# Attention over a key/value cache: one of five P tiles of every second step transposed by DMA instead of TensorE

## Chip, core and metric

The kernel runs on one core of a Trainium2 chip. The metric is the device time of one execution in microseconds; a lower time is better. The kernel before takes 722.17 us, the median of three runs (721.92 to 722.21).

## What is computed

Two independent problems, A and B, of the same shape are computed, and their outputs are set side by side. All arrays are bf16.

```python
# x (16, 80, 576), k_cache and v_cache (16, 16, 512, 128), wq (576, 4096), wo (4096, 576)
q = (x @ wq).reshape(16, 80, 32, 128).transpose(0, 2, 1, 3)     # 32 query heads
k, v = jnp.repeat(k_cache, 2, axis=1), jnp.repeat(v_cache, 2, axis=1)   # 16 cached heads, 2 query heads each
p = softmax(einsum("bhqd,bhkd->bhqk", q, k) * 128 ** -0.5)
o = einsum("bhqk,bhkd->bhqd", p, v)
out = o.transpose(0, 2, 1, 3).reshape(16, 80, 4096) @ wo         # (16, 80, 576)
```

## The kernel before

The work is cut into 128 steps, numbered U: one step is one batch element with four cached heads (so eight query heads) of one problem. Its 8 x 80 = 640 query rows make five tiles of 128 rows by 512 keys. Tiles k = 1 to 4 hold the first 128 of the 160 rows of each cached head. Tile k = 0, the remainder tile, holds the last 32 rows of each of the four heads, 4 x 32 = 128 rows. A step goes through these operations:

- The K load (`em_ldk`, L626) is a transposing DMA for two steps at once, into one of six buffers (`NK`); the V load (`em_ldv`, L630) is a plain DMA for one step. Both are issued by SyncE (SP), as are the loads of `wq`, `wo`, `x` and the stores of the output (`em_st`, L851).
- The query projection (`em_qp`, L537) multiplies `wq` by the transposed `x`. The last 64 of the 576 rows of the contraction are done by `em_qt` (L550) as two matmuls on the two 64-row halves of the array, side by side. A projection that belongs to a step U of at least `US0` has its `em_qt` pair put at the head of that step's transposes; an earlier one is an instruction pair of its own.
- The scores are `em_qk` (L673, full array, 512 columns) for tiles 1 to 4 and `em_qkr` (L660, four 32-column strips) for the remainder tile. From the third step on the remainder tiles of two neighbouring steps are scored together.
- The softmax of a tile is a maximum on VectorE (L682), an exponential with its row sum on ScalarE (L686), a reciprocal on VectorE (L692), for tiles 0 to 2 and 3 to 4 together, and the normalisation on GpSimd (POOL, `em_nrm`, L695), which writes the P tile in SBUF.
- The transposes (`em_tr`, L727) turn the five P tiles on TensorE into PSUM: 40 instructions, in pairs on the two 64-row halves of the array. Two copies per step (`em_ptev`, L738 on ScalarE or L740 on VectorE) bring tiles 1 to 4 into `pT` in SBUF, and two more (`em_prev`, L745 or L747) bring the remainder tile. `pT` has two blocks (`NPT`), used by even and odd steps.
- P·V (`em_pv`, L770) is four groups of four matmuls with V as the stationary and 160 columns of `pT` as the moving operand. The result goes to `oT` (L784).
- The output projection (`em_op`, L816) multiplies `oT` by `wo`; copies and additions (L828, L845) and the stores end it.

Nothing is scheduled at run time. Every operation is added to a list with its engine, the tiles it reads and writes, and a stream name, and the table `ORDER` gives the order of all of them, with the PSUM bank of each result and, where an apostrophe stands, ScalarE in place of VectorE for a copy. The letters stand for the streams in alphabetical order. Each engine takes its operations in that order. Waits on semaphores are derived from the reads and writes, and every DMA waits in SP's one queue:

```python
for op in ops:
    if op.eng != name:
        continue
    for ck, v in op.waits:
        e.wait_ge(sem_of(ck), v)
    inst = op.emit(e, name) if op.alt else op.emit(e)
```

Of the kernel before, what the change touches and what calls it, by code (L numbers as in the profile page):

```python
# [18 lines left out]
NPT = 2  # L19
# [11 lines left out]
US0 = 2  # L31
# [16 lines left out]
XLD = ((-100.0, -60.0), (-5.0, -4.9))  # L48
# [11 lines left out]
LETTERS = "abcdefghijklmnopqrstuvwxyzABCDEFGHIJKLMNO"  # L60
ORDER = """
nEKni7KHHHHHHNj3Ej4IMk5j6MNIj7j3Mk4ILd6Id5IIdd2AaBd1dd5BAd6dd2'Bd1dd6BMd0AdAd7'BAd5Ldd4'A'Bd6dd5'ABKMd7add3'AB
d4e0doe1'Be2'Ad5ole7of6ld3ole0pe1dlod4omd2Ke7A'BhdCloe6vhf5Cald3oud0lBupf12luAdme7puo'BOmg0456Cpu'Ae1y'wOe3'xl
vj0oj4d5'zuCMj7loe6ud0moue1dMlk2Md4Llok7e2c3'AFBcle6hod5a'sLldog0137'BAe2'yCd5CCvw'zoj3e0lue7Mj4o'xve3lc6Mcuc1
locuof24ld0tu'spc7lucpg16muCtme3uzd2'youe7e6'wd4'xho'AFlg15oalBc3Cz'xe0u'wcle7Bc5uoc'yf46v'ACsle1oud2'tpd3ulc5
omcpg07lCsuc4'yCze1e5'wvmcob7u'Aolue0te2'xe6olhud4hoblholae0Bd5lCove1f23'qolug67Cplud0wumzc1cpu'yc7e2'Axe6smcd
4o'BCg13olutle5uc2xCco'zue7c6'sBd3vlwoe2e4u'ycCod5'Aulhtc1e0huoclag67sloe1'zc2yc'xlCf47Coud6'tBv'wle0pe2c5uAcm
c1ouc'se3od4'tulpg15vlob0'wCyluxe2'zAue1bomhColaue6e7d3oluc5Be2'qocle0d4Colug16sluof57'zvyd2lCpc6u'wc'xp'Ae0uc
1md3Bo'tcmg45hF'se6'yxe1hCBc7u'zFe4oclae5vb3olute0lwboolc7Ce1olud6Acluc4qcCovd3se0ulg25Cou'tf17'yxuCBe4'zd2wvp
lc3d5uAmoe0ucpg16'sulob3wlze4A'ye6bhCouholavc2d1q'xulcd3tme0Bf26og45plpc7mcyd0'wme2sc4oc'ze7d6C'txulBc4cou'Ae5  # L70
c3'socle1g24o'thlChCe7uxb3'who'yua'Ae2le5uoe0b'zuolCe1Bd4ulod6vloc7ue2lCqcc5ovlcg03slCtvf17y'zue2'xCb3p'Buwmpc
6ucAbmuo'sue0le1hoc7ud4'qhold3hae2lcCovg56'tluf01y'zub7w'xCpu'Be2Ambuople0c3oc'qc4'se2d5loce7C'td3vole0ug46lub
2'zCymohb'wJxBGe1'qc7oJcle2hc3Ald4hoe0acClod5vsg16lu'tuf27C'zwyb3u'xpuc6AmcuBe0e1oe4uc5bsloc'qd6tle0od3oe1lg25
olCb4pu'zxmwue0ye5blvABd6oc7ohle1e2Jqd3lGochg04slJof57a'w'yAc1pcb6'tCCx'zvle0d4uo'Be1c2umocd3ule5buloCslug01Cp
'quc2w'x'ye6Aue5cmod4u'zte0d7o'Ble1og23loc6'wCcylud5az'sue2'Ac0xe6lCocuc3'BcCv'toc4e1lcuod7'tlsuf02lg34upmb6y'
zwhpe0'xd3'AaComue1e5c4Blvcoc2c'svod7lute0le4og12ole5bxz'ylCoe0ud2'w'BAc4ule1Cod3v'qhcolc7uhe6Chcloug05h'tsuhl
f17xauB'ye4e6p'wb3'zpmc5od0mocle1Ad7slg24CouCc6'yzvce5'xC'te2wvd4ole6oulboule1Bc5ulAce2oud7'qoc3ulcCsg06lu'tuf
15z'w'ye2pb3'x'Bhomc7hCAculae0e1od4ubplComuc6e0qd2luog35slCuf17x'yBc'wu'zpe0d3'tomc5cCpc6u'Ae2le1scvod4'tvog05
lhuhle6zb2a'yCoume1we0vod5'x'Bc7Aulcoc4cld3t'se6e1log47ole0bCCo'wulzud6'x'yBe1u'Ae7Coc4ld3uo'qe5hvclag02sulof1
4u'wxlAc7cp'yb6p't'ze0e7moe2c5cBlbCouod3lvCc1slue0qcd5omuhhf27tlug46pe0y'wb1'zC'xou'Be6mFbvolue2qc4'Ae5olcac3s  # L80
d1CCpcud4'toulg06vb3'wzluA'xue2me6Bboyld4oe1Fc7od5lhqg02lf36'wz'Ae1xcCoc4u'sce2Blhud7od5'tp'ye1Ke4lob0mCoue2bl
puolvg13lc4z'ycc2q'se1acmoe0e4b3xlCCou'td6Bulwd2ovg15AluCf07w'zCve4'ype5b'AuomFoue1lKc6xd0uKo'qe4lhd3uolcuBc5c
# [184 lines left out]
def bass_concat_heads__gqa_block_cached__gqa_block_cached__near_ridge_kernel(  # L267
# [27 lines left out]
    with ExitStack() as es:  # L295
# [634 lines left out]
```

## Time and profile before

| | |
|---|---|
| median of three runs | 722.17 us |
| the profiled execution | 722.56 us |
| its span, first to last instruction | 720.6 us |
| TensorE clock granted | 1.0 of full speed |
| TensorE matmuls busy | 715.3 us (99%) |
| VectorE, ScalarE, GpSimd busy | 641.3, 639.8, 432.6 us |
| DMA bytes moved | 160.73 MB, mean 223 GB/s |

The profile is one execution. An engine's busy time is the time in which it had an instruction in work; matmuls overlap in TensorE's pipeline, so the mean time of one is longer than the distance from one to the next. "Idle before" is the time for which an engine had nothing in work before an instruction, with the engine and line that ended it. The chain of the profile follows the work back from the last instruction, at each step to what released it. For a DMA, the issue is the time of the instruction in SP's queue, and the landing is counted from the start of the issue to the semaphore.

### The profile page before, as it was taken

The numbers are of one execution on the slowest core, as the hardware profiler recorded it, in microseconds if no ns is written. First come the engines' busy times: TensorE is split into PE (matmuls) and PEld (weight loads), VectorE is DVE, ScalarE is ACT, GpSimd is POOL, SyncE is SP. The second block draws the span as 40 slices with busy tenths as digits, with TensorE's granted clock in tenths as the row PEclk, the third lists the DMA queues.
The fourth block names the chain that finished last, engine by engine and source line by source line (L and its number), as shares of the span: only waits on it lengthen the run. The fifth ranks groups of instructions, "written<-read, shape, count | busy, mean of one in ns | idle before, by whom it ended". The sixth has DMA issues, their size and how long they took to land.

```text
span 720.6 us, 26290 instructions
## 1 busy us (share of the span) xinstructions
PE 715.3 (99%) x10820; PEld 513.1 (71%) x10820; DVE 641.3 (89%) x1459; ACT 639.8 (89%) x1844; POOL 432.6 (60%) x650
## 2 busy tenths in 40 slices
PE   9999999999999999999999999999999999999998
PEld 5567767777677777777777777777777777777777
DVE  3999998899888998899998899979999889998995
ACT  1999999799989998789997899989999889998993
POOL 0477755566556675665675567646676656755773
PEclk9999999999999999999999999999999999999999
DMA  9999999899999999999999998999999898988860
GB/s 248 268 269 259 265 255 241 206 189 259 225 241 209 217 254 240 226 254 205 268 207 219 248 245 212 247 236 204 181 262 224 193 241 198 220 194 200 178 199 18
DMA packets 374167, 160.73 MB, mean 223 GB/s; under 512 B 278560, under 2 KB 370976, under 8 KB 374048
## 3 DMA queue, kind: packets, MB, share of 16 engines
q1 hardware_dynamic: 374048, 159.05, 95.6%
q8 instruction: 86, 1.41, 0.8%
q14 instruction: 33, 0.27, 0.1%
HBM read 87.65 MB, written 2.95 MB: 126 GB/s over the span
## 4 chain that ended last, share of the span: by engine, by line
PE 98%; ACT 1%; issue 0%; DVE 0%
PE ps L816 22%; PE ps L770 20%; PE ps L537 19%; PE ps L673 16%; PE ps L727 11%; PE ps L660 5%; PE ps L550 4%; ACT p_sb L686 1%; PE ps L348 0%; PE ps L396 0%; ACT qT L563 0%; PE ps L414 0%; PE ps L451 0%; DVE osb L845 0%; DVE wo_sb L341 0%
## 5 line engine op out<-in xcount | busy, mean ns | idle before, releaser
L695 POOL TENSOR_SCALAR p_sb<-p_sb,rinv 128x512 bf16<-128x512 bf16 x640 | 430.8, 694 | 272.7 <-DVE rinv L692 272.2
L686 ACT ACTIVATE p_sb<-ps,negmax 128x512 bf16<-128x512 f32 x640 | 444.0, 711 | 29.8 <-DVE negmax L682 25.5
L682 DVE TENSOR_REDUCE negmax<-ps 128x1 f32<-128x512 f32 x640 | 419.2, 681 | 27.5 <-PE ps L673 22.2
L770 PE MATMUL ps<-pT,v_sb 128*128 128x160 bf16 x2048 | 191.1, 233 | 0.1
L770 PEld LDWEIGHTS ps<-pT,v_sb 128*128 128x128 bf16 x2048 | 154.0, 98 | 39.5 <-ACT pT L745 3.3
L816 PE MATMUL ps<-wo_sb,oT 128*128 128x288 bf16 x1280 | 181.6, 286 | 0.0
L673 PE MATMUL ps<-kT,qT 128*128 128x512 bf16 x512 | 176.4, 381 | 0.0
L537 PE MATMUL ps<-xT,wq_sb 128*128 128x320 bf16 x1024 | 176.0, 299 | 0.0
L816 PEld LDWEIGHTS ps<-wo_sb,oT 128*128 128x128 bf16 x1280 | 122.1, 98 | 43.2 <-ACT p_sb L686 1.7
L686 ACT ACTIVATION_READ_ACCUMULATOR p_sb<-ps,negmax 128x1 f32 x640 | 144.0, 225 | 0.0
L537 PEld LDWEIGHTS ps<-xT,wq_sb 128*128 128x128 bf16 x1024 | 94.5, 98 | 42.4 <-ACT p_sb L686 2.2
L727 PEld LDWEIGHTS ps<-ident,p_sb 64*128 64x128 bf16 x5120 | 91.4, 95 | 8.8 <-issue 1.1
L727 PE MATMUL ps<-ident,p_sb 64*128 64x64 bf16 x5120 | 96.1, 190 | 1.2 <-ACT qT L563 0.7
L738 ACT COPY pT<-ps 128x512 f32<-128x512 f32 x150 | 88.4, 603 | 9.4 <-PE ps L727 9.0
L740 DVE COPY pT<-ps 128x1024 bf16<-128x1024 bf16 x106 | 72.0, 684 | 13.2 <-PE ps L727 11.7
L563 ACT ACTIVATE qT<-ps 128x320 bf16<-128x320 f32 x131 | 59.5, 462 | 16.2 <-PE ps L550 15.4
L784 DVE CAST oT<-ps 128x320 bf16<-128x320 f32 x129 | 61.5, 482 | 6.5 <-PE ps L770 6.0
L564 DVE TENSOR_SCALAR qT<-ps 128x320 bf16<-128x320 f32 x125 | 59.5, 482 | 8.1 <-PE ps L550 6.6
L673 PEld LDWEIGHTS ps<-kT,qT 128*128 128x128 bf16 x512 | 48.4, 97 | 25.7 <-issue 3.3
L784 ACT CAST oT<-ps 128x320 bf16<-128x320 f32 x127 | 56.4, 448 | 10.2 <-PE ps L770 9.9
L745 ACT COPY pT<-ps 128x128 f32<-128x128 f32 x132 | 36.1, 288 | 7.0 <-PE ps L727 6.8
L692 DVE RECIPROCAL rinv<-rowsum 128x3 f32<-128x3 f32 (+1 forms) x256 | 39.5, 161 | 2.3 <-ACT p_sb L686 2.2
(31 smaller groups left out, 194.7 us busy)
## 6 DMA issues: line engine op xcount, KB each, us to landing
v_sb<-in_A_v_cache_dram SPq DMA_DIRECT2D x64, 512.0 KB, 5.4
v_sb<-in_B_v_cache_dram SPq DMA_DIRECT2D x64, 512.0 KB, 4.9
wo_sb<-in_A_wo_dram SPq DMA_DIRECT2D x8, 576.0 KB, 5.6
wo_sb<-in_B_wo_dram SPq DMA_DIRECT2D x8, 576.0 KB, 5.6
wq_sb<-in_B_wq_dram SPq DMA_DIRECT2D x4, 1024.0 KB, 6.6
out_dram<-osb SPq DMA_DIRECT2D x40, 72.0 KB, 3.4
wq_sb<-in_A_wq_dram SPq DMA_DIRECT2D x8, 256.0 KB, 4.5
wq_sb<-in_A_wq_dram SPq DMA_DIRECT2D x2, 1024.0 KB, 7.3
```

Source lines behind the costliest of these rows:

```text
L537: last = e.matmul(ps[:, vbq[h].phys, QO:QO + 320], lhsT=wq_sb[:, wsl, ck, hi * 128:(hi + 1) * 128], rhs=xT[:, half, ck, n0:n0 + 320], star ...
L563: return e.activation(dst, src, AF.Identity, scale=SCALE)
L673: return e.matmul(ps[:, vb.phys, :], lhsT=qT[:, qsl, bl, gl * 160:gl * 160 + 128], rhs=k_of(U, gl), start=True, stop=True)
L682: return e.tensor_reduce(negmax[:, si:si + 1], ps[:, vb.phys, :], axis=AX.X, op=AluOpType.max, negate=True)
L686: return e.activation(p_sb[:, psl, :], ps[:, vb.phys, :], AF.Exp, bias=negmax[:, si:si + 1], scale=1.0, accum_out=rowsum[:, ss, k:k + 1])
L695: return e.tensor_scalar(p_sb[:, psl, :], p_sb[:, psl, :], rinv[:, ss, k:k + 1], 1.0, op0=AluOpType.mult, op1=AluOpType.mult)
L727: last = e.matmul(dst, lhsT=p_sb[64 * h:64 * h + 64, psls[k_], j * 128:(j + 1) * 128], rhs=ident[64 * h:64 * h + 64, 64 * h:64 * h + 64], ...
L738: return e.copy(pT[:, pts, :, :].bitcast(F32)[:, :, 32 * h:32 * h + 32], ps[:, vtp[h].phys, :].rearrange("p (n c) -> p n c", n=16))
L740: return e.tensor_copy(pT[:, pts, :, 64 * h:64 * h + 64], psb[:, vtp[h].phys, :].rearrange("p (n c) -> p n c", n=16))
L770: last = e.matmul(ps[:, vo.phys, off:off + 160], lhsT=v_sb[:, vs, gl, j * 128:(j + 1) * 128], rhs=pT[:, pts, 4 * gl + j, :], start=(j == 0 ...
L784: return (e.copy if en == "act" else e.tensor_copy)(dst, src)
L816: last = e.matmul(ps[:, vb.phys, 0:DC], lhsT=oT[:, sp_ * (HH // 2) + i, rb * 128:(rb + 1) * 128], rhs=wo_sb[:, 2 * c3 + sp_, i, :], start= ...
```

## The change

In the 52 odd steps from 21 to 123 (`RT0`, `RT1`, `RTM`, `RT2`) the remainder tile is not transposed by TensorE. A DMA transpose, `em_rtr`, issued by SP, takes it from `p_sb` to `pT`. The transposes of these steps are 32 instructions, they need no PSUM bank for the remainder tile unless the step carries a projection, and the two `em_prev` copies are left out.

For this, `pT` is laid out anew in every step. Before, a row of `pT` was 16 groups (cached head, key block) of 160 contiguous columns. Now it is four key blocks of five sub-blocks of 128 columns: four sub-blocks hold tiles 1 to 4 cut by 32 rows, so that P·V takes five runs of 32 columns with a step of 128, and the fifth sub-block is the remainder tile as it is. All transposes of tiles 1 to 4 write two runs of 32 columns in PSUM, as those of the remainder tile did before. `US0` goes from 2 to 0, so that the `em_qt` pairs of steps 0 and 1 stand with those steps' transposes. The other early `em_qt` pairs have a stream of their own (`QT`), and in the new order five of them stand in runs of two and three. `XLD` moves an early load of `x` in the list, and the table `ORDER` is another one throughout.

```diff
-US0 = 2
+US0 = 0
+RT0 = 21
+RT1 = 125
+RTM = (0, 1)
+RT2 = 999
...
-XLD = ((-100.0, -60.0), (-5.0, -4.9))
+XLD = ((-100.0, -85.0), (-5.0, -4.9))
...
-        pT = sb("pT", [128, NPT, 16, 160], BF16)
+        pT = sb("pT", [128, NPT, 4, 5, 128], BF16)
...
+            rtr = RT0 <= U < RT1 and (RTM[U % 2] or U >= RT2)
+            vtq = td["vb"] if td else [] if rtr else [S.bank() for _ in range(2)]
...
-                for n_ in range(20):
+                for n_ in range(4 if rtr else 0, 20):
                     k_, j = divmod(n_, 4)
                     for h in range(2):
                         if k_:
-                            c_ = ((k_ - 1) * 4 + j) * 64
-                            dst = psb[:, vtp[h].phys, c_:c_ + 64]
+                            dst = psb[:, vtp[h].phys, 256 * j:256 * j + 256].rearrange("p (i n) -> p i n", i=2)
+                            dst = dst[:, :, 32 * (k_ - 1):32 * k_]
                         else:
-                            dst = psb[:, vtq[h].phys, 0:256].rearrange("p (g j c) -> p g j c", g=2, j=4)[:, :, j, :]
+                            dst = psb[:, vtq[h].phys, 64 * j:64 * j + 64]
...
+            if rtr:
+                def em_rtr(e, psl=psls[0], pts=pts):
+                    return e.dma_start_transpose(pT[:, pts, :, 4, :], p_sb[:, psl, :])
+
+                S.add("sp", 5.0 * U - 0.4, em_rtr, reads=[R(("P", psls[0]), ("n", 5 * U))],
+                      writes=[R(("pR", pts, h), U) for h in range(2)], dsem="d_r%d" % pts, name="rtr%d" % U, stream="RT")
...
+                    dst = pT[:, pts, :, 2 * h:2 * h + 2, :].rearrange("p j i n -> p j (i n)")
...
-                S.add(en, ts + 0.45 + 0.1 * h, em_prev, reads=[R(vtq[h], 0)],
-                      writes=[R(("pR", pts, h), U), R(("tb", pts, h), U)], name="prev%d.%d" % (U, h), stream="prev%d" % h, alt=EV)
+                if not rtr:
+                    S.add(en, ts + 0.45 + 0.1 * h, em_prev, reads=[R(vtq[h], 0)],
+                          writes=[R(("pR", pts, h), U), R(("tb", pts, h), U)], name="prev%d.%d" % (U, h), stream="prev%d" % h, alt=EV)
...
-                                        rhs=pT[:, pts, 4 * gl + j, :], start=(j == 0), stop=(j == 3))
+                                        rhs=pT[:, pts, j, :, 32 * gl:32 * gl + 32], start=(j == 0), stop=(j == 3))
```

More of the change, by code (lines that the diff above doesn't have):

```diff
@@ L322, in bass_concat_heads__gqa_block_cached__gqa_block_cached__near_ridge_kernel @@
                      + ["d_out%d" % i for i in range(NOSB)]
+                     + ["d_r%d" % i for i in range(NPT)]
                      + ["d_k%d" % i for i in range(NK)] + ["d_v%d" % i for i in range(NV)])
@@ L730, in em_tr @@
                 return last
-            S.add("pe", ts, em_tr, reads=[R(("P", psls[k_]), ("n", 5 * U + k_)) for k_ in range(5)] + [IDENT]
+            if rtr:
[3 more added lines that the diff above has]
+                      writes=[R(("pR", pts, h), U) for h in range(2)], dsem="d_r%d" % pts, name="rtr%d" % U, stream="RT")
+            S.add("pe", ts, em_tr, reads=[R(("P", psls[k_]), ("n", 5 * U + k_)) for k_ in range(1 if rtr else 0, 5)] + [IDENT]
                 + (td["reads"] if td else []),
```

155 lines of the change are left out of this document (75 added, 80 removed).

## The prediction

> **What bounds the kernel now.** I read the page first: engine shares, the chain that ended last, the DMA queue.
>
> ```profile
> PE 715.3 (99%) x10820; PEld 513.1 (71%) x10820; DVE 641.3 (89%) x1459; ACT 639.8 (89%) x1844; POOL 432.6 (60%) x650
> ...
> q1 hardware_dynamic: 374048, 159.05, 95.6%
> ...
> PE 98%; ACT 1%; issue 0%; DVE 0%
> ```
>
> TensorE is 98% of the chain, so the kernel lasts as long as TensorE's instructions take one behind the other. A busy share of 99% alone would not say that, since matmuls overlap in their pipeline. So next I read what TensorE waited for, in the groups by line, where the last columns are the idle time before a group and what ended it.
>
> ```profile
> L727 PE MATMUL ps<-ident,p_sb 64*128 64x64 bf16 x5120 | 96.1, 190 | 1.2 <-ACT qT L563 0.7 <-issue 0.6
> L770 PE MATMUL ps<-pT,v_sb 128*128 128x160 bf16 x2048 | 191.1, 233 | 0.1
> L816 PE MATMUL ps<-wo_sb,oT 128*128 128x288 bf16 x1280 | 181.6, 286 | 0.0
> L673 PE MATMUL ps<-kT,qT 128*128 128x512 bf16 x512 | 176.4, 381 | 0.0
> L745 ACT COPY pT<-ps 128x128 f32<-128x128 f32 x132 | 36.1, 288 | 7.0 <-PE ps L727 6.8
> L747 DVE COPY pT<-ps 128x256 bf16<-128x256 bf16 x124 | 33.5, 282 | 8.7 <-PE ps L727 7.9
> ```
>
> The matmul queue stood still for 1.2 us before transposes and 0.1 us before P·V; no row of it names a DMA. What is taken from TensorE's stream comes off the span, as long as nothing new makes it wait. The engines beside it (VectorE and ScalarE 89%) wait for TensorE, not it for them.
>
> **Transposes removed.** In 52 steps (odd U, 21 to 123) the remainder tile's 8 of 40 transposes go: 416 instructions. Their price is their spacing, not the 190 ns of one. The timeline of one step, TensorE alone:
>
> ```profile
> 304.04 0.31 PE L550 MATMUL ps<-xT,wt 64*128 64x320 bf16 x2
> 304.19 0.75 PE L727 MATMUL ps<-ident,p_sb 64*128 64x64 bf16 x40
> 304.87 0.62 PE L660 MATMUL ps<-kT,qT 128*32 128x512 bf16 x8
> 305.41 1.04 PE L673 MATMUL ps<-kT,qT 128*128 128x512 bf16 x4
> ```
>
> Forty run in 0.75 us from first start to last end; less one's 0.19 us, over 39 spacings, that is 14.4 ns each. 416 x 14.4 ns = 6.0 us. The remaining 32 stay in the same row-tiled stretch, so nothing else of it goes.
>
> **Stretches merged.** Rows of the chain (start, length, what):
>
> ```profile
> 12.57 1.19 PE ps L537 x8
> 14.01 1.19 PE ps L537 x8
> 37.52 1.11 PE ps L770 x16
> 46.48 1.09 PE ps L537 x8
> 280.04 1.96 PE ps L816 x16
> ```
>
> Early on, eight projection matmuls and one row-tiled pair (L550) repeat every 14.01 - 12.57 = 1.44 us. The eight alone take 1.09 us, and the pair, 320 columns side by side, about one of them, 0.14 us. So going into row tiles and back costs 0.21 us. The new order merges such stretches: two pairs move into the transposes of steps 0 and 1 (US0 = 0), five others of the prelude stand in runs of two and three. Counted on TensorE's instruction order, stretches of L550, L660 and L727 between full-array matmuls fall from 150 to 141: 9 x 0.21 = 1.9 us. Together 7.9 us less TensorE work.
>
> **P·V and the transposes write and read another layout.** P·V's moving operand was 160 contiguous columns and is now 5 runs of 32; 2048 matmuls. No moving operand with such short runs is in the trace; the nearest is the scores' (L673), four runs of 128. From 160 to 288 contiguous columns the mean goes from 233 to 286 ns, 0.414 ns a column; on to 512 that would be 379, and L673 has 381. So a join costs 0 to 0.8 ns, and four joins in 2048 matmuls 0 to 6.6 us. I take 0: the 2 ns are as likely L673's own, and nearer to 0 than to anything that counts. Below 0 is excluded, a contiguous read cannot be beaten by a broken one. PSUM writes of 2x32 were already those of the remainder transposes, inside the same 0.75 us. The copies out of PSUM keep their element counts (runs of 128 in place of 32 words on ScalarE): nothing, and their cover is VectorE's and ScalarE's 11% of idle time.
>
> **Copies removed.** 104 remainder copies of 282 to 288 ns, 30 us over two engines, are off the chain: worth nothing directly; they give the eviction behind a transpose some room. New copies, waits or instructions on those engines there are none, only another order.
>
> **What is added: 52 DMA transposes of 128 KB on SP's queue.** Each waits for the normalised remainder tile (POOL, L695) and for P·V of step U-2, which read the same pT block; P·V of U waits for its landing, and TensorE works in order, so all behind that P·V stands too. While SP waits, the loads of K and V queued behind it stand. The trace has no SBUF-to-SBUF transfer and no transpose of this size. The rows of SP's issues (issue duration min/median/max, then landing), the K loads, V loads and output stores:
>
> ```profile
> L626 SPq DMA_TRANSPOSE kT<-in_A_k_cache_dram x32: 3947/5826/9546, 9.3 to 330.0; - x32
> ...
> DMA to landing us min/median/max: 6.3/8.6/13.1
> L630 SPq DMA_DIRECT2D v_sb<-in_A_v_cache_dram x64: 367/544/1632, 21.9 to 354.6; - x64
> ...
> DMA to landing us min/median/max: 3.8/5.2/9.0
> L851 SPq DMA_DIRECT2D out_dram<-osb x40: 332/503/1682, 237.0 to 718.5; - x40
> ...
> DMA to landing us min/median/max: 1.6/3.4/6.0
> ```
>
> And from the page's list of DMA issues (KB each where shown, median us to landing):
>
> ```profile
> xT<-in_B_x_dram SPq DMA_TRANSPOSE x2, 7.5
> ...
> wt<-in_A_wq_dram SPq DMA_DIRECT2D x8, 64.0 KB, 4.4
> ```
>
> Bounds for issue to landing: 1.6 us (the fastest 72 KB store) and 7.5 us (the smaller transposing load, 640 KB). In size the new one is next to the 64 KB load (4.4) and the store (3.4), and K against xT, 8.6 - 7.5 us for 384 KB more, adds 0.4 us for 128 KB. I take 4.0 us.
>
> What it has: the work that the new order puts on TensorE between the last P·V of U-2 and the first of U. The tightest is U = 77: four scores (each (1.04 - 0.38)/3 = 0.22 us), four projections (0.54), its L550 pair and 32 transposes with one stretch (0.14 + 0.47 + 0.21), and 16 P·V (1.11): 3.3 us. Counted so for all 52, windows under 4, 5, 6 us are 2, 4 and 9, and the median is 8.8. The sum of what a landing of 4.0 us lacks is 0.8 us; of 5.0, 3.4; of 5.5, 6.2; of 6.3, 13.6. Walking SP's queue in the new order along TensorE's work, with a K load holding it for its median 5.8 us and a V load for 0.5, SP comes late to 32 of the 52, by 1.5 us in the median, and the sums are 2.1, 8.0, 13.5 and 27.9. Between 0.8 and 2.1 I take 1.5 us. The remainder tile itself is early: for odd U it is scored together with that of U-1, a step ahead.
>
> K and V behind it: SP has time to spare, since it waits for free buffers:
>
> ```profile
> SPq L626 <- PE ps L673: 140.7, 21, 9.5
> SPq L626 <- PE ps L770: 78.6, 12, 9.0
> ```
>
> 52 issues take 28 us at a V load's 0.54 each, the nearest in bytes, and 203 us at most, at K's fastest 3.9; these two rows alone hold 219 us of waiting. DMA traffic grows by 6.8 MB of 159 (4%) on a queue marked 95.6%; I cost that at nothing; the cover is that K has six buffers (NK), so a load is issued while two other pairs are still there to be scored. If that cover goes somewhere, a K load is late: at the worst by the 4.5 us between its median landing and the longest, once.
>
> **Sum.** The profiled execution took 722.56 us (span 720.6 and 2.0 around it): 722.6 - 7.9 + 1.5 = 716.2. The median of the runs is 0.4 us lower, so 715.8 us.
>
> **Rivals.** (1) Landing in queue order. For 33 of the 52 the instruction just ahead on SP is a V load, which lands 5.2 us after an issue that takes 0.54. If the new transfer can't pass it, it lands 5.2 - 0.5 + 0.4 = 5.1 us after its own issue: between 4 and 9 us of waiting by the two counts, 6.4 in the middle, 720.7 us. For: V's median is well over its minimum of 3.8, so loads do stand behind each other. Against: many V loads ahead are issued early, and are over when SP has waited. The Trainium skill, DMA: Bandwidth & Descriptors, section Queues, rings and completion order, has it so: each DMA engine takes the descriptors of one ring in ring order. By that rule the time is this rival's 720.7, by the rows of small transfers 715.8.
>
> (2) Slower: every transposing DMA of this trace lands after 6.3 us or more. If that is a property of transposing and not of the 640 KB and more that they carry, then the lack is 14 to 28 us, 21 in the middle: 735 us. The point is a landing of 5.0 to 5.7 us by the two counts, where the lack is 7.9 us and the gain gone. For: 6.3 to 13.1 is all that transposing has shown here. Against: the issue alone is 3.9 us or more of it, and should take less for an eighth of the bytes.
>
> (3) Joins in P·V's operand cost their bound of 6.6 us: 722.4.
>
> (4) The new order starves TensorE elsewhere (a late K load, an eviction at the start, where P·V of step 0 now follows its transposes by 1.4 us): up to 4.5 us, 720.3. That the change does not do what it says has no chance: the 416 transposes are gone from the instruction order.
>
> **How the numbers follow.** The forecast 0.54; rival 1 0.17; 2 0.17; 3 0.05; 4 0.07. A measurement of this kernel can tell 0.2%, 1.4 us. Faster by more: the forecast, 0.10 of rival 1, 0.01 of 3, 0.04 of 4: 0.69. Slower: rival 2, 0.03 of 1, 0.02 each of 3 and 4: 0.24. Within it: 0.07. The range begins at 713.0, where no landing is late (7.9 less) and TensorE's present 1.2 us of waiting goes as well, and reaches to 724.0, where the landings lack 9.7 us: beyond lies most of rival 2, 0.15, below 0.04.
>
> **What would show it.** Right: the transposes' line with 4704 instructions and TensorE's idle time before P·V still around 1 us; P·V's mean at 233 ns; the new DMA at 3 to 5 us to landing. Rival 1 shows as waits of P·V for a DMA of pT, a few us in all; rival 2 as many, with landings over 5.6; rival 3 as a P·V mean of 235 to 236 ns; rival 4 as waits of L673 for kT. The prediction is wrong if TensorE's idle time grows by over 6 us, or if the stretches' 1.9 us do not come.

## The result, and the profile after

| kernel | median, us (range) | ratio to the kernel before, 95% interval |
|---|---|---|
| before, run beside it | 721.95 (720.8 to 723.87, 12 runs) | |
| after | 725.62 (723.19 to 731.6, 12 runs) | 1.0064 (1.0037 to 1.0091) |

The change makes the kernel slower by 0.6%, where 0.9% faster was forecast; the result lies 1.6 us above the range. The profiled execution took 729.1 us (span 727.4), 3.5 us over the median; the spread of the runs has grown from 3 to 8 us.

The page of the changed kernel: engine shares, the DMA queue, the chain by engine.

```profile
PE 710.9 (98%) x10404; PEld 506.2 (70%) x10404; DVE 628.4 (86%) x1413; ACT 632.1 (87%) x1786; POOL 433.9 (60%) x650
...
q1 hardware_dynamic: 402336, 165.87, 103.5%
...
PE 87%; DMA 5%; ACT 4%; DVE 1%; SPq 1%; issue 1%; ACTq 0%; DVEq 0%
```

TensorE has 416 matmuls fewer, as meant, and is busy for 4.4 us less. But its share of the chain fell from 98% to 87%; DMA and ScalarE hold 9% of it, 65 us. That share tells where the chain runs, not what the change costs: while it runs through ScalarE, TensorE mostly has other work. In the groups by line (mean of one, then TensorE's idle time before the group) the idle time is found where before there was 0.1 and 0.0 us:

```profile
L780 PE MATMUL ps<-pT,v_sb 128*128 128x160 bf16 x2048 | 192.2, 233 | 6.4 <-issue 2.8
...
L677 PE MATMUL ps<-kT,qT 128*128 128x512 bf16 x512 | 178.2, 380 | 4.7 <-ACT p_sb L690 4.7
...
L541 PE MATMUL ps<-xT,wq_sb 128*128 128x320 bf16 x1024 | 173.5, 299 | 1.1 <-DMA wq_sb<-in_A_wq_dram 1.0
...
L732 PE MATMUL ps<-ident,p_sb 64*128 64x64 bf16 x4704 | 89.5, 190 | 0.0
```

P·V (L780) keeps its 233 ns in the new layout, but stands for 6.4 us. For 2.8 us of it the row names nothing that was waited for ("issue"). Two stops, of 1.9 us before P·V of step 25 and 1.6 us before that of step 59, end 0.1 us after the landing of that step's transfer, so they are put down to it; 1.3 us stand before P·V of steps 0 and 6, ahead of the first transfer. The scores (L677) stand for 4.7 us, and not for a load of K, which the forecast's fourth rival would have shown: for the exponentials on ScalarE (L690). What ScalarE waits for is told by the waits of all engines (us in total, times, the longest):

```profile
ACT p_sb L690 <- DMA pT<-p_sb: 11.3, 7, 4.2
PEld ps L677 <- ACT p_sb L690: 10.6, 18, 3.1
...
DVE osb L855 <- DMA out_dram<-osb: 1.7, 1, 1.7
```

The waits of SP's own queue, which issues every DMA, for K buffers (L630) and ahead of the new transfers (L739):

```profile
SPq L630 <- PE ps L677: 114.1, 18, 8.0
SPq L630 <- PE ps L780: 109.2, 18, 8.9
...
SPq L739 <- POOL p_sb L699: 25.4, 19, 2.5
...
SPq L739 <- PE ps L677: 14.8, 10, 3.7
```

And the new transfer's own line, issue duration and landing:

```profile
L739 SPq DMA_TRANSPOSE pT<-p_sb x52: 1188/1195/2290, 141.7 to 700.4; - x52
...
DMA to landing us min/median/max: 2.4/4.7/6.9
```

So there are three ways from a late transfer to TensorE. The first is the forecast's: P·V of U waits for the landing. The second is in the first row of the waits: the remainder tile of P has four slots (`NPR`), and the exponential of step U+4 may not overwrite a slot until the transfer has read it. ScalarE stands 11.3 us for that, seven times; scores already made are not taken out of PSUM, and TensorE has no bank for the next. The timeline around step 33's transfer (start, length; idle time before in brackets):

```profile
204.40 1.19 SPq L739 DMA_TRANSPOSE pT<-p_sb  x1
...
208.52 0.72 PE L780 MATMUL ps<-pT,v_sb 128*128 128x160 bf16 x8
...
210.60 0.69 ACT L690 ACTIVATE p_sb<-ps,negmax 128x512 bf16<-128x512 f32 x1 [4.23 <-DMA pT<-p_sb]
...
212.11 0.39 PE L677 MATMUL ps<-kT,qT 128*128 128x512 bf16 x1 [2.87 <-ACT p_sb L690]
```

The transfer is issued at 204.40 and lands just ahead of 210.60; ScalarE stands 4.23 us, TensorE 2.87 us behind it.

The third way is SP's queue: what stands behind a waiting or slow instruction there is late. Two stores of the output, seen at the VectorE addition that fills the `osb` slot (L855) and at SP, and then the next user of the slot:

```profile
287.11 5.22 SPq L630 DMA_TRANSPOSE kT<-in_A_k_cache_dram  x1
292.38 0.58 SPq L634 DMA_DIRECT2D v_sb<-in_A_v_cache_dram  x1
293.00 0.98 SPq L861 DMA_DIRECT2D out_dram<-osb  x2
```

```profile
298.58 0.46 DVE L855 TENSOR_TENSOR osb<-ps,acc 128x288 bf16<-128x288 f32 x1 [1.71 <-DMA out_dram<-osb]
...
299.67 0.69 ACT L690 ACTIVATE p_sb<-ps,negmax 128x512 bf16<-128x512 f32 x1 [2.07 <-DVE negmax L686]
...
300.51 0.39 PE L677 MATMUL ps<-kT,qT 128*128 128x512 bf16 x1 [0.68 <-ACT p_sb L690]
```

The additions ended by 289.2 us, their stores are issued from 293.00 on, behind a K load that held SP for 5.22 us; the next addition stands 1.71 us for the slot, the maximum behind it on VectorE is late, so is the exponential, and TensorE stands 0.68 us. The kernel before has no wait of an addition for a store at all. But no transfer stands directly ahead of these stores. In the trace of the kernel without the transfers (below), whose order is otherwise the same, the same K load holds SP for 4.82 us; the second store is issued 4.0 us after its addition, here 4.4, and lands 3.9 us after its issue, here 4.9; the next addition stands 0.3 us there. So it is the order that leaves this store little room; with the transfers it lands 1.4 us later still.

### The profile page after: what moved, and what is told of

Same layout as the page of the kernel before. It is cut to its first block, busy times and chain, and to the rows that moved or that the text cites. A ratio compares the mean times of both kernels' runs of the same rounds, so it can differ in the third digit from the quotient of the medians.

```text
span 727.4 us, 25472 instructions
## 1 busy us (share of the span) xinstructions
PE 710.9 (98%) x10404; PEld 506.2 (70%) x10404; DVE 628.4 (86%) x1413; ACT 632.1 (87%) x1786; POOL 433.9 (60%) x650
## 4 chain that ended last, share of the span: by engine, by line
PE 87%; DMA 5%; ACT 4%; DVE 1%; SPq 1%; issue 1%; ACTq 0%; DVEq 0%
PE ps L826 20%; PE ps L780 19%; PE ps L541 17%; PE ps L677 14%; PE ps L732 9%; PE ps L664 4%; DMA pT<-p_sb 4%; PE ps L554 4%; ACT p_sb L690 3%; DMA wq_sb<-in_A_wq_dram 1%; DVE negmax L686 1%; DMA out_dram<-osb 1%; ACT qT L567 0%; ACT pT L750 0%; SPq L506 0%
## 5 line engine op out<-in xcount | busy, mean ns | idle before, releaser
L690 ACT ACTIVATE p_sb<-ps,negmax 128x512 bf16<-128x512 f32 x640 | 443.1, 710 | 42.4 <-DVE negmax L686 28.1
L780 PE MATMUL ps<-pT,v_sb 128*128 128x160 bf16 x2048 | 192.2, 233 | 6.4 <-issue 2.8
L780 PEld LDWEIGHTS ps<-pT,v_sb 128*128 128x128 bf16 x2048 | 153.3, 98 | 49.5 <-issue 7.2
L677 PE MATMUL ps<-kT,qT 128*128 128x512 bf16 x512 | 178.2, 380 | 4.7 <-ACT p_sb L690 4.7
L541 PE MATMUL ps<-xT,wq_sb 128*128 128x320 bf16 x1024 | 173.5, 299 | 1.1 <-DMA wq_sb<-in_A_wq_dram 1.0
L690 ACT ACTIVATION_READ_ACCUMULATOR p_sb<-ps,negmax 128x1 f32 x640 | 143.3, 224 | 0.0
L750 ACT COPY pT<-ps 128x512 f32<-128x512 f32 x161 | 94.0, 599 | 14.1 <-PE ps L732 13.5
L732 PEld LDWEIGHTS ps<-ident,p_sb 64*128 64x128 bf16 x4704 | 85.3, 95 | 7.3 <-ACT p_sb L690 1.0
L732 PE MATMUL ps<-ident,p_sb 64*128 64x64 bf16 x4704 | 89.5, 190 | 0.0
L794 DVE CAST oT<-ps 128x320 bf16<-128x320 f32 x138 | 66.0, 481 | 9.5 <-PE ps L780 8.7
L751 DVE COPY pT<-ps 128x1024 bf16<-128x1024 bf16 x95 | 64.9, 684 | 10.4 <-PE ps L732 9.6
L677 PEld LDWEIGHTS ps<-kT,qT 128*128 128x128 bf16 x512 | 48.0, 97 | 28.3 <-ACT p_sb L690 10.6
L568 DVE TENSOR_SCALAR qT<-ps 128x320 bf16<-128x320 f32 x121 | 57.2, 482 | 10.5 <-PE ps L554 7.0
L794 ACT CAST oT<-ps 128x320 bf16<-128x320 f32 x118 | 51.3, 443 | 4.3 <-PE ps L780 4.0
L664 PE MATMUL ps<-kT,qT 128*32 128x512 bf16 x512 | 39.6, 384 | 0.2 <-ACT oT L794 0.2
```

The costliest lines, as they stand in the source:

```text
L541: last = e.matmul(ps[:, vbq[h].phys, QO:QO + 320], lhsT=wq_sb[:, wsl, ck, hi * 128:(hi + 1) * 128], rhs=xT[:, half, ck, n0:n0 + 320], star ...
L664: last = e.matmul(ps[32 * g4:32 * g4 + 32, vb_.phys, :], lhsT=qT[:, qsl_, bl_, g4 * 160 + 128:g4 * 160 + 160], rhs=k_of(U_, g4), start=Tru ...
L677: return e.matmul(ps[:, vb.phys, :], lhsT=qT[:, qsl, bl, gl * 160:gl * 160 + 128], rhs=k_of(U, gl), start=True, stop=True)
L690: return e.activation(p_sb[:, psl, :], ps[:, vb.phys, :], AF.Exp, bias=negmax[:, si:si + 1], scale=1.0, accum_out=rowsum[:, ss, k:k + 1])
L732: last = e.matmul(dst, lhsT=p_sb[64 * h:64 * h + 64, psls[k_], j * 128:(j + 1) * 128], rhs=ident[64 * h:64 * h + 64, 64 * h:64 * h + 64], ...
L750: return e.copy(dst.bitcast(F32), ps[:, vtp[h].phys, :].rearrange("p (j n) -> p j n", j=4))
```

## The experiments

The kernel before is compared on the same chip each time; its medians in the seven lots of runs were 721.3 to 722.0 us. All edits are of the changed kernel where nothing else is said.

**One wait away, or both.** In the first kernel the P·V of the 52 steps does not wait for the landing, in the second the P slot is not held until it, the third has both edits. What is left out is the remainder rows of these steps.

```diff
 # first: P·V of the 52 steps reads 160 columns of blocks 0 and 1, and nothing that the transfer writes ("pR")
-  reads=[R(("V", vs), U)] + [R((n_, pts, h), U) for n_ in ("pT", "pR") for h in range(2)],
+  reads=[R(("V", vs), U)] + [R((n_, pts, h), U) for n_ in (("pT",) if rtr else ("pT", "pR")) for h in range(2)],
-  rhs=pT[:, pts, j, :, 32 * gl:32 * gl + 32]
+  rhs=pT[:, pts, j, 0:2, :].rearrange("p i n -> p (i n)")[:, 0:160] if rtr else pT[:, pts, j, :, 32 * gl:32 * gl + 32]
 # second: the transfer reads wq_sb; it still waits for the normalisation
-  return e.dma_start_transpose(pT[:, pts, :, 4, :], p_sb[:, psl, :])
+  return e.dma_start_transpose(pT[:, pts, :, 4, :], wq_sb[:, wsl_, 0, 0:512])
```

> The DMA transposes stay, with the same waits, but P·V of the 52 steps reads 160 other columns of pT (blocks of tiles 1 and 2) and so does not wait for the landing; the remainder rows of those steps are left out. Theory 1 (P·V waits for the landing): 720 us, some 5.5 us under the changed kernel's 725.6. Theory 2 (the P slot is held until the landing, ScalarE's exponential of step U+4 waits for it): 724 to 725.5, as the slots are still held. Theory 3 (the new order starves TensorE by itself): 725.6.

> The DMA transposes stay, with the same waits, and P·V waits for them, but they read 512 columns of wq_sb in place of the P tile, so that the P slot is free once it is normalised; the remainder rows of those steps are left out. Theory 1: 725, no change. Theory 2: 720.5 us, as ScalarE's 11.3 us of waiting for the DMA go. Theory 3: 725.6.

> Both edits at once: the 52 transfers run, and nobody waits for them but the next transfer. The remainder rows of those steps are left out. Theories 1 and 2 together: 716 to 717 us, about what was forecast. Theory 3: 725. If the traffic or SP's time itself delays K: in between, with waits of the scores for kT.

Measured: 729.5 us without the wait of P·V (1.0120, 1.0099 to 1.0141), 726.8 without the wait of the slot (1.0075, 1.0052 to 1.0097), 722.7 without both (1.0009, 0.9994 to 1.0024). Neither wait alone is the cause: with one gone, late transfers still come through the other. With P·V's wait gone the row of ScalarE's waits is about what it was (11.3 us, seven times):

```profile
ACT p_sb L690 <- DMA pT<-p_sb: 9.6, 9, 4.0
```

With both gone 2.9 us of 725.6 go. 7 us are left over the kernel in which the transfers are not issued (715.7 us, next paragraph), though neither P·V nor ScalarE waits for a transfer any more. No theory had 729.5 us for the first kernel. For the second, "no change" is within the intervals. The third lies between the two theories, but without the waits for `kT` that were to show it (0.3 us).

That the first kernel is slower than the changed one goes with the granted clock, of which each run lists the mean. All six of its runs have a mean below 1.00 (0.995 to 0.998), as have four of the changed kernel's twelve; compared among these, the medians are 729.5 and 729.8 us. The profiles show how that comes. At the same wait for step 33's transfer, TensorE stood 2.87 us in the changed kernel and went on at full clock (the score at 212.11 took 0.39 us, against a mean of 0.38). With P·V's wait gone it stood 2.67 us, and then the clock was halved for 3.4 us:

```profile
209.00:213.00 4.00, 3.03 (x40) 1.62 (x40) 1.58 (x3) 2.85 (x10) 0.00 (x0) 0.57 1.11 318
```

This line gives start and end, length, the busy time of TensorE's matmuls, its weight loads, VectorE, ScalarE and POOL, then TensorE's granted clock, the DMA share and GB/s.

**The transfers not issued.**

```diff
-  S.add("sp", 5.0 * U - 0.4, em_rtr, reads=[R(("P", psls[0]), ("n", 5 * U))], ...
```

> As before, and the 52 transfers are not issued at all (the remainder rows of those steps are left out). Theories 1 and 2: 715 to 716.5 us, within 1 us of the run with the transfers. Theory 3: 724 or more. What stays over 714.2 (722.1 less 7.9) is what the order itself costs, at the start above all, where the projections now wait for wq.

Measured: 715.66 us (0.9920, 0.9907 to 0.9933), as expected. So everything in the change but the 52 transfers gains 5.8 us, and the transfers cost 725.6 - 715.7 = 9.9 us, where the forecast had 1.5.

**The transfers issued, but SP waits for nothing ahead of them.** Like the kernel with both waits gone, and further:

```diff
-  reads=[R(("nd", U), 0), R(("wq", wsl_, 0), None), R(("wq", wsl_, 1), None), R(("pvd", U - 2), 0)]
+  reads=[R(("wq", wsl_, 0), None), R(("wq", wsl_, 1), None)]
```

> As the kernel in which neither the P.V steps nor the P slots wait for the 52 transposing transfers (722.7 us), but now SP also issues them without waiting: they read a slot of wq_sb as there and nobody reads what they write, and the wait for the normalisation and for P.V of U-2 ahead of them is gone. The remainder columns of those 52 steps are left out of P.V's input, so the output is not the reference's. Theory Q (the queue's head): what was left of the cost there, 722.7 - 715.7 = 7 us, is SP standing at a transfer's wait with the stores and loads of the table queued behind it (stores late, so the two osb slots late, so VectorE's additions late; K and wt loads late). Then the time is 716 to 718 us. Rival T (traffic): the 52 transfers and their 1.2 us of issue each take SP's and the DMA rings' time by themselves: then it stays at 720 to 723 us.

Measured: 718.53 us (0.9952, 0.9940 to 0.9964), half a microsecond above the end of Q's range and 4.2 us below the kernel in which SP still waits. The transfers land no sooner than there, by the rows of the two kernels (both waits gone, then nothing waited for):

```profile
L741 SPq DMA_TRANSPOSE pT<-wq_sb x52: 1188/1216/2254, 141.4 to 690.9; - x52
...
DMA to landing us min/median/max: 2.4/5.1/7.6
```

```profile
L741 SPq DMA_TRANSPOSE pT<-wq_sb x52: 1194/1228/2462, 141.6 to 686.5; - x52
...
DMA to landing us min/median/max: 2.4/5.2/7.8
```

So these 4.2 us come of SP's standing and not of a slower DMA. By the medians the 9.9 us are then 2.9 us for the transfers' own time on SP and in the ring (718.5 - 715.7), 4.2 us for SP standing ahead of them (722.7 - 718.5), and 2.9 us for those who wait for the landing (725.6 - 722.7). By the intervals each of the three is uncertain by 1 to 2 us. Part of the first may be the edit's own: as the transfers read `wq_sb`, SP waits for that tile here, 16 us in four waits.

The clock moves the split too. Among the runs at a mean granted clock of 1.00 alone it is 2.9, 1.5 and 4.3 us:

| kernel | median of all runs, us | of the runs at clock 1.00, us |
|---|---|---|
| changed | 725.6 (12 runs) | 724.4 (8) |
| both waits gone | 722.7 (12) | 720.0 (4) |
| SP waits for nothing either | 718.5 (5) | 718.5 (5) |
| not issued | 715.7 (4) | 715.7 (4) |

So the size of the transfers' cost is well shown, 9 to 10 us, and so is that it has these three parts; how large SP's standing is apart from the halved clock that long stops bring is not.

**SP's order anew.** Order table only; SP's instructions around step 61, old and new:

```diff
- st0.1.0 ldv58 ldv59 rtr57 ldv60 ldk62 ldk64 ldv61 rtr59 ldv62 ldk66 ldv63 rtr61 st0.1.1 ldv64 st0.1.2 ldk68
+ st0.1.0 ldk60 rtr57 ldv57 ldk62 ldv58 ldv59 st0.1.1 ldv60 ldv61 rtr59 ldk64 rtr61 ldk66 ldv62 ldv63 st0.1.2
```

> The changed kernel, nothing left out, with the order of SP's instructions alone anew from step 21 on (149 of its 340 stand elsewhere among their neighbours; every other engine's order and all banks are as they were): each remainder transfer is issued ahead of the K and V loads that used to stand ahead of it, and those loads, which have 10 us and more before their use, come behind it; stores stay where they have time. Worked out with the landings measured in the changed kernel (a remainder transfer lands 2.4 us after its issue with nothing ahead of it in the ring, and 0.55 us behind the last load ahead of it otherwise) 18 of the 52 transfers land after their first need in the old order and 2 (steps 21 and 23) in the new one. Theory R (the landing behind loads in one ring is the cause of all three routes: P.V, the P slot, the queue's head): 716 to 719 us, 1.002 times the 715.7 of the kernel without the transfers, and faster than the kernel before (721.5). Rival W (the windows between the normalisation and the first need are too short even for prompt landings, or the loads that were held back now come late): 722 us or more.

> As the kernel with SP's order anew, and at the start the load ldwa0.3 back ahead of ldwa1.0, as in the kernel before. Theory S (of the 7.9 us less work on TensorE some 2 us do not come because the merged stretches of the start wait for the wq_sb loads that the new order of SP brings later): 0.5 to 1.5 us less than the same kernel without this. Rival: the start is bound by the loads whatever their order, then the two are within 0.3 us.

Measured: 732.3 us (1.0144, 1.0130 to 1.0158) and, with the load of the start moved too, 730.4 (1.0126, 1.0103 to 1.0149). Theory R fell in this form. The loads that had to give way come late themselves; the waits of the first of the two kernels:

```profile
ACT p_sb L690 <- DMA pT<-p_sb: 7.3, 9, 2.8
...
DVE osb L855 <- DMA out_dram<-osb: 5.0, 4, 1.9
...
PE ps L780 <- DMA pT<-p_sb: 2.0, 1, 2.0
...
PE ps L780 <- DMA v_sb<-in_A_v_cache_dram: 0.9, 1, 0.9
```

ScalarE's wait fell from 11.3 to 7.3 us, but that for the stores rose from 1.7 to 5.0, and P·V now also waits for a load of V. One bad place shows in SP's timeline:

```profile
319.15 7.64 SPq L435 DMA_TRANSPOSE xT<-in_B_x_dram  x1
326.83 0.58 SPq L441 DMA_DIRECT2D xst<-in_B_x_dram  x1
327.46 0.52 SPq L861 DMA_DIRECT2D out_dram<-osb  x1
328.02 0.44 SPq L634 DMA_DIRECT2D v_sb<-in_A_v_cache_dram  x1
328.50 1.30 SPq L440 DMA_DIRECT2D xst<-in_B_x_dram  x1
329.84 0.43 SPq L634 DMA_DIRECT2D v_sb<-in_A_v_cache_dram  x1
330.38 1.19 SPq L739 DMA_TRANSPOSE pT<-p_sb  x1
```

The long issue of 7.64 us (2.4 to 3.6 us in the changed kernel and in the two in which nobody waits for the landing) holds six instructions, the transfer last. The windows around it, with the columns explained above, show what it does to TensorE:

```profile
330.00:333.00 3.00, 3.00 (x31) 2.10 (x27) 2.92 (x7) 2.94 (x9) 2.89 (x5) 1.00 0.87 258
333.00:335.70 2.70, 0.09 (x1) 0.00 (x0) 1.08 (x3) 0.00 (x0) 2.70 (x5) 0.95 1.35 196
335.70:339.10 3.40, 3.31 (x43) 3.03 (x45) 0.94 (x2) 2.87 (x8) 0.01 (x1) 0.54 1.27 286
339.10:342.00 2.90, 2.90 (x52) 2.13 (x43) 2.67 (x8) 2.12 (x7) 0.00 (x1) 1.00 0.78 127
```

TensorE stands for 2.7 us, and is then granted a clock of 0.54 for the next 3.4 us, in which it does about half: another 1.6 us lost, by an estimate from these two numbers. The load of the start told nothing here, the two kernels' ranges overlap.

**Fewer transfers in the changed order.** Steps named in a list, the copies of the others put back beside their neighbours:

```diff
-RTM = (0, 1)
-RT2 = 999
+RTS = (27, 33, 35, 37, 39, 41, ..., 123)          # 41 steps; in a second kernel 25
-rtr = RT0 <= U < RT1 and (RTM[U % 2] or U >= RT2)
+rtr = U in RTS
```

> The changed kernel with eleven of the 52 remainder tiles (steps 21, 23, 25, 29, 31, 45, 55, 71, 77, 85, 87: those with the shortest stretch between the normalisation and the first need, or in the stretch to step 29 in which the ring is never empty) transposed on TensorE again, with their two copies; nothing left out, SP's order otherwise as it was. TensorE has 11 x 8 x 14.4 ns = 1.3 us more to do, so without any waiting 715.7 + 1.3 = 717.0 us. Theory F (few transfers with short windows make most of the waiting): 719 to 722 us. Rival G (the waiting comes from the queue as a whole, each transfer that goes leaves its place to the next one): 723 to 726 us, as the changed kernel.

> As the kernel with 41 transfers, and SP's order from step 21 on anew: an order in which, by the landings measured in the runs so far (remainder 2.45 us alone, 0.62 us behind a load, and 0.6 us more for the V or wo load behind it; K 6.6 us alone, V 4.5 us), each remainder transfer and each load lands 3 us ahead of its first need where the places allow it, not 0.7 us as in the first attempt at a new order (732 us). Theory R (order, with margin): 717.5 to 720 us. Rival W (the loads that give way come late themselves, whatever the margin): 723 us or more.

> The changed kernel with 25 of the 52 remainder tiles by DMA (33, 41, 43, 47, 49, 51, 53, 57, 63, 79, 81, 83, 89, 91, 97, 99, 101, 103, 105, 111, 115 and the four from 117 on: most of them have over 6 us between readiness and first need) and 27 on TensorE again, with their copies; nothing left out. Work on TensorE: 715.7 + 27 x 0.115 = 718.8 us; the transfers' own 2.9 us, 25/52 of it, 1.4 us: 720.2 us when nobody waits for them. Theory F (the waiting comes from the transfers with short windows): 720 to 721.5 us. Theory G (the waiting goes with the number of transfers: 8.4 us at 52, 7.0 at 41 over the sum of the work): about 4.3 us over 718.8, 723 us.

Measured: 724.0 us with 41 (1.0036, 1.0024 to 1.0048), 728.5 with 41 and SP's order anew (1.0099, 1.0068 to 1.0131), 730.7 with 25 (1.0124, 1.0108 to 1.0140). The first is where G had it; all its runs are at clock 1.00, where the changed kernel has 724.4 us, so eleven transfers fewer are worth 0.3 us there. The trace of the second, of a run of 724.1 us, shows 3.0 us of waiting for `kT`; its three runs at clock 1.00 take 723.9 to 726.8 us and the three below it 730.1 to 731.7. The third is worse than either theory had it. It tells nothing on the transfers: nobody in its trace waits for one. What has grown is the wait of one copy for another; the rows of VectorE's q copy for ScalarE's remainder copy (L756), in the changed kernel and in the one with 25:

```profile
DVE qT L568 <- ACT pT L756: 2.1, 3, 0.9
```

```profile
DVE qT L568 <- ACT pT L756: 8.1, 13, 1.0
```

I take it that the changed order has no room for the 54 copies put back into it, and that the q copies, which free PSUM banks, stand behind them. That is argued and not tested, and 6 us more of this wait do not account for all of the 12 us over the sum of the work.

**A third slot for the stores.**

```diff
-NOSB = 2
-NS = 32
-NSS = 6
+NOSB = 3
+NS = 8
+NSS = 3
```

> The changed kernel with three osb slots in place of two (NS 8 for 32, NSS 3 for 6 to make room), all else as it was. Theory Q (part of the cost comes through stores that stand behind a waiting transfer in SP's order, VectorE's addition waiting for the slot, and scores' banks behind that): 1 to 3 us less than the changed kernel's 725.6, so 722.5 to 724.5 us. Rival: those waits lie beside others, then 725 to 726 us.

> As the kernel with 41 transfers and SP's new order, with three osb slots in place of two for the output stores (room for it from fewer negmax and rowsum slots: NS 8 for 32, NSS 3 for 6). Theory: where stores are issued late because they stand behind a transfer that waits, VectorE's addition for the next block no longer waits for the slot: 0.5 to 2 us less than the same kernel with two slots. Rival: the stores cost nothing here, within 0.3 us; or fewer rowsum slots add waits of ScalarE, then slower.

Measured: 734.5 us (1.0181, 1.0148 to 1.0215) and 734.7 (1.0180, 1.0167 to 1.0194), 9 and 6 us slower than with two slots. The wait for the stores got longer, 6.6 us where it was 1.7:

```profile
DVE osb L855 <- DMA out_dram<-osb: 6.6, 3, 2.7
```

A slot more does not help where the store itself is late at SP. Why it costs so much is open in the main. Both profiles have two stretches of 3.4 us at half clock, which by themselves cost about 3.4 us; the fewer `negmax` and `rowsum` slots may have a part in it, though no wait for them stands out.

**The start.** On the kernel without transfers, whose runs spread by 1 us only, the first 80 entries of the order table as in the kernel before, so that early row-tile pairs stand alone again: 145 stretches by the trace, where the merged start has 141 and the kernel before 150.

```diff
- ... qp0.2.0 qp0.2.1 qt0.1 qt0.2 ... qp1.2.0 qp1.2.1 qp1.3.0 qp1.3.1 qt1.1 qt1.2 qt1.3 ...
+ ... qp0.2.0 qp0.2.1 qt0.2 qp0.3.0 qp0.3.1 qt0.3 ... qp1.2.0 qp1.2.1 qt1.2 qp1.3.0 qp1.3.1 qt1.3 ...
```

> The kernel without the 52 transfers (not issued; the remainder columns of those steps are left out of P.V's input; 715.7 us), with the first 80 entries of the order table, to the first two projections of the second row block (about 20 us of the run), as in the kernel before, banks renamed to fit: the early pairs of row tiles one after the other again, and SP's loads in the earlier order. Theory S (the batched start waits for its wq_sb and K loads, 2.3 us at qp0.0.0, qp0.1.0, qp0.3.0 and qk1 in that kernel's trace against under 0.5 us in the kernel before, more than its merged stretches save): 713.5 to 714.7 us. Rival M (what is not waited for there is waited for at the next place, or the merged stretches save as much): 715.3 to 716.5 us.

Measured: 715.72 us (0.9921, 0.9908 to 0.9935) against 715.66. That is rival M, though the two intervals leave room for a difference of 1 us and more. The traces show the reason. With the stops left out, TensorE's instructions take 707.1 us from start to next start with the merged start and 708.1 us with the old one: the four stretches cost 1.0 us of work, 0.25 us each. But the stops are 2.9 and 1.8 us. The merged start is shorter, and the projections then wait for the loads of `wq`; in the kernel without transfers, merged,

```profile
PE ps L541 <- DMA wq_sb<-in_A_wq_dram: 1.0, 2, 0.7
```

and with the old start 0.4 us in that row; 0.7 us more of waiting for `kT` is gone too. With this start, the kernel with 25 transfers took 730.6 us against 730.7, the same again:

> As the kernel with 25 transfers, with the start (first 80 entries of the table) of the kernel before. Theory S: 1 to 2.2 us less than the same kernel with the changed start, and so 719 to 720.5 us by F, at the edge of being faster than the kernel before (721.3); by the rival M no less than that kernel.

**The layout alone, and transfers in the order of the kernel before.** The last four kernels keep the order of the kernel before. One has only the new layout of `pT`; three have a few transfers with long windows, each put into SP's order where the landings measured so far leave room, and the copies of those steps left out.

```diff
 # in before's order, US0 = 2; kernel with 23
+RTS = (52, 57, 59, 61, 66, 68, 70, 78, 79, 82, 83, 84, 89, 91, 94, 95, 97, 101, 102, 104, 110, 113, 114)
+rtr = U in RTS
```

> The kernel before with the new block layout of pT alone (remainder tiles in a block of their own, P.V's operand as runs of 32 columns out of five blocks), all transposes on TensorE, order and copies as before. Forecast's step (c), no cost: 721.1 to 721.9 us. Rival 3 (joins in P.V's moving operand): up to 6.6 us more.

> The kernel before, its order of work kept (banks, start, every engine's order), with the new block layout of pT and 27 remainder tiles by DMA: steps 52, 57, 59, 61, 66, 67, 70, 74, 78, 79, 82, 83, 84, 86, 89, 91, 93, 94, 95, 97, 101, 102, 103, 104, 110, 113, 114, odd and even ones, taken where the trace of the kernel before leaves 5 us and more between readiness (normalised, P.V of U-2 done) and first need, and where by the measured landings the transfer comes 2 us early and no load or store behind it comes later than its need less 1.5 us. Their copies are gone, nothing is inserted but the transfers. TensorE 27 x 0.115 = 3.1 us less; the transfers' own cost, 27/52 of the 2.9 us of the kernel in which nobody waits, 1.5 us more. Theory F (what costs is short windows): 721.5 - 3.1 + 1.5 = 719.9 us, 719.3 to 720.7. Theory G (each transfer on SP's queue costs (725.6 - 715.7) / 52 = 0.19 us whatever its window, more than the 0.115 us that it saves): 723.5 us.

> As the kernel with 27 transfers in the order of the kernel before, with 14 (steps 52, 57, 66, 67, 70, 74, 94, 97, 101, 102, 104, 106, 110, 113: windows of 7.4 us and more, 3 us early by the measured landings). TensorE 1.6 us less, the transfers' own cost 0.8 us more. Theory F: 720.7 us. Theory G: 721.5 + 14 x 0.075 = 722.6 us.

> As the kernel with 27 transfers in the order of the kernel before (720.3 us), with 23 (52, 57, 59, 61, 66, 68, 70, 78, 79, 82, 83, 84, 89, 91, 94, 95, 97, 101, 102, 104, 110, 113, 114), taken so that besides the transfers being 2.5 us early no K load comes later than its need less 4 us and no store later than its need less 5 us: in the trace with 27 nobody waits for a transfer any more, but 1.2 us go to a store that stands behind a K load and transfers, and 0.7 us to the K load of step 92. TensorE 4 x 0.115 = 0.5 us more than with 27, those 1.9 us gone at best, the transfers' own cost 0.2 us less: 718.7 us at best, 720.3 to 720.8 if others take their places. Theory H (the queue's head is what is left): 718.7 to 719.8. Rival: 720 to 721.

Measured: layout alone 721.93 us (1.0003, 0.9994 to 1.0012); 27 transfers 720.31 (0.9984, 0.9973 to 0.9996); 14 transfers 720.82 (0.9988, 0.9978 to 0.9997); 23 transfers 720.13 (0.9978, 0.9969 to 0.9987). The layout is free within these 0.1%. 27 and 14 are where F had them and G had not: in this order, transfers with room around them save a little. That it is the missing room and not the other order that makes the 52 lose is not separated by a run: no kernel has the short windows in this order. In the trace with 23 nobody waits for a landing, although the landings take up to 6.5 us:

```profile
L739 SPq DMA_TRANSPOSE pT<-p_sb x23: 1189/1192/1769, 310.7 to 645.9; - x23
...
who waited for it (us, times):
busy tenths in 40 slices 0000000000000000000000000000000000000000
DMA to landing us min/median/max: 2.4/3.9/6.5
```

What I wanted of 23 against 27, that the waits behind SP's head go, did not come (720.1, in the rival's range); the additions still wait 2.0 us for a store, and 0.5 of TensorE's gain is given back. Still, of those that compute everything this kernel has the lowest median, 0.2% under the kernel before by an interval that leaves out 1; from the kernel with 27 it cannot be told apart.

## Why the prediction was wrong

**TensorE's work: 7.9 us less.** As work it came: with the stops left out, TensorE's instructions take 715.1 us from start to next start in the trace before and 707.1 us in that without the transfers, and the transposes still start 14.3 ns apart. As time only 5.8 us came. The term "Stretches merged", 1.9 us, is what failed, and by the test the text gave for it: it left out that a shorter start waits for its loads. The start waits for `wq` (1.0 us in the changed kernel, no such row before); the trace without the transfers reaches the P·V of step 12, ahead of every removed transpose and after nearly the same matmuls, 1.4 us later than the trace before, and putting the old start back changed 0.06 us.

**Layout and copies.** The layout at 0, against a bound of 6.6 us: right, 0.3 us with an interval on both sides of none, and 233 ns for P·V; rival 3 falls. That the removed copies are "worth nothing directly" has no test of its own; the kernel with 25 transfers, 12 us over the sum of its work, suggests that in this order they cannot be put back for nothing.

**The transfers: 1.5 us.** This is the step that failed, with 9.9 us measured, at three places.

First, the landing, taken as 4.0 us: it was 4.7 us in the median and 2.4 to 6.9. Rival 1 was right on it. Four traces (the changed kernel, each wait gone, both gone) have 208 transfers. For 106 of them the last to land of those ahead in the queue, mostly a load, landed 4 to 6 us after their own issue; they landed 0.53 us after that one in the median (middle half 0.49 to 0.60). The two with nothing ahead of them landed after 2.4 us. The rule that the prediction cited from the Trainium skill, DMA: Bandwidth & Descriptors, section Queues, rings and completion order, agrees with these landings. By the forecast's own walk, between its sums for 4.0 and 5.0 us, a landing of 4.7 us lacks about 6 us. With that alone the forecast would have been under 2 us faster.

Second, only P·V was asked for as one who waits. The source tile's slot was not: "The remainder tile itself is early" spoke of when it is ready and not of when its slot must be free. And it is not always early: in the trace without transfers 18 of the 52 are normalised only after the P·V of U-2, by 2.1 us in the median. Of the 52 windows between readiness and first need there, 28 end at the exponential of U+4, not at P·V, and the median of all is 6.2 us where the forecast counted 8.8 to P·V. Taking away either wait alone gained nothing; in the changed kernel's trace both end at the same landing in steps 25, 59 and 71.

Third, "K and V behind it: SP has time to spare, since it waits for free buffers". SP does: in the two largest rows it still stands 114.1 and 109.2 us for K buffers after the change, 223 us, where it was 219 before. But that is a sum over the run. A queue issues in order, and the next store behind the instruction that stands has some 8 us of room, its landing included (289.2 to 296.9 us in the lines above), and not 219. SP's standing costs 4.2 us by the medians, 1.5 us among the runs at full clock; which stores and loads carry it was not tested one by one. About 2.9 us more go to the transfers' own issue (1.2 us each, 62 us in all; the forecast's lower bound was 28, from a V load that it calls the nearest in bytes, though the 72 KB store is nearer) and their time in the ring, also costed at nothing; no run tells these two apart.

**The range** ended at 724.0 where the landings lack 9.7 us, with rival 2 (735 us) above it. The transfers cost 9.9 us, so the size of the lack at the range's end was met, but by luck: only the part for those who wait for the landing (2.9 us, or 4.3 at full clock) is what that term counted. And against it stand 5.8 us, not 7.9. Rival 2's landings of 6.3 us and more came in five of the 52.

**The signs to look for** were well chosen: 4704 transposes, P·V at 233 ns and landings of 3 to 5 us (in the median) came, and "TensorE's idle time grows by over 6 us" is what told the miss: 6.4 and 4.7 us in two groups, 0.1 and 0.0 before.

## What to carry to other kernels

A transfer that replaces work on the bound engine has two clients: whoever reads what it writes, and whoever next writes what it reads; count the window to the earlier of the two. An in-order DMA queue's slack is not its total waiting time but the room of the next instruction behind the one that stands, stores and small loads included. Move only the pieces whose windows are longer than the slow landing behind the loads in the ring: here 23 well-placed transfers gain 0.2%, while 52, in another order, lose 0.6%.

## What was not expected of the hardware

- A transposing DMA of 128 KB from SBUF to SBUF takes 1.19 us to issue (a median of 52, at most 2.29) and lands 2.4 us after its issue at the least; behind a transfer that is still to land it lands 0.53 us after that one (a median of 106).
- After TensorE had stood still for 2.7 us, the granted clock was 0.54 over the next 3.4 us (the windows shown above). Such a wait then costs more than half as much again. The Trainium skill, TensorE: Matmul & The Clock Gate, section Part 1: The HAM clock gate, gives half clock after an idle window of about 3.4 us; here 2.7 us were enough, and the half clock lasted 3.4.
- The length of the stop alone does not decide it: the 2.87 us of the changed kernel brought no half clock. Within the run, six kernels' traces have eight half-clock stretches, each of 3.41 us. Where a trace has two, they start 474.45 and 498.34 us apart, which is 139.00 and 146.00 times 3.4133 us. Cut each trace into pieces of that length, counted from its half-clock stretch: TensorE stands for 1.95 to 3.00 us in the piece just before a stretch, and for at most 1.84 us in every other piece after the first 30 us of the run. By these traces, then, a stop that lies across the border of two pieces can pass without harm. It shows in the runs too: with both waits for the landing gone, the four at a mean clock of 1.00 take 719.6 to 720.8 us, and the eight below it 722.2 to 724.6.
